# Second-layer output tiles in two tag groups, and one block of the second DFT in other PSUM banks

## The chip, the cores and the metric

The kernel runs on one core of a Trainium2 chip. The core has five engines that work through their own instruction streams in order: TensorE (PE, matrix products), VectorE (DVE), ScalarE (ACT), GpSimd (POOL) and SyncE (SP, which here only issues transfers). They wait for one another through semaphores. On-chip memory is SBUF, 128 partitions wide; matrix products go to PSUM, used here in units called banks (one bank holds 128 x 512 values of 4 bytes). The metric is the device time of one execution in microseconds (us); lower is better.

## What is computed

The reference is one transformer-like block with two branches, on a sequence of 4096 tokens with 640 channels:

```python
h = _layernorm(x) * (1 + ca) + sa
x = x + ga * _A_ref(h, A_w1, A_b1, A_w2, A_b2)     # spectral branch
h = _layernorm(x) * (1 + cb) + sb
x = x + gb * _B_ref(h, B_w_gate, B_w_up, B_w_down) # SwiGLU FFN
```

where `sa, ca, ga, sb, cb, gb` come from `silu(c) @ w_mod`, and the spectral branch is

```python
Xf = rfft2(x, axes=(1, 2))                  # H is 1: a 4096-point real DFT per channel
z  = Xf.reshape(B, H, Wf, NB, BS)           # 4 blocks of 160 channels
hr = zr @ w1[0] - zi @ w1[1] + b1[0]        # complex layer 1, per block; then ReLU
hi = zi @ w1[0] + zr @ w1[1] + b1[1]
or_ = hr @ w2[0] - hi @ w2[1] + b2[0]       # complex layer 2, per block
oi_ = hi @ w2[0] + hr @ w2[1] + b2[1]
...
mr = abs(or_) - lam                         # soft threshold, lam = 0.01
or_ = sign(or_) * mr * (mr > 0)
...
irfft2(or_ + 1j * oi_)
```

The change concerns the spectral branch alone.

## The kernel before

**Stages.** The 4096-point DFT is split as 128 x 32. In the first stage the x tiles (`xa0` to `xa7`, 128 partitions x 4 x 640 values, 10,240 bytes per partition each) are normalised and transformed over the 128 direction by TensorE; the results go back into the same x tiles and from there to memory (`write_s1`, lines 352 and 355; line 355 is used for tiles 6 and 7 only). Those writes are in three groups (f = 0, 1, 2), since different frequency chunks need different rows. The order in which they are issued on SP's queue is written out by hand: group 0 first, then group 1, then group 2, where tiles 6, 7 and 0 come last, in this order.

In the second stage the frequencies are done in 8 chunks of 256 (chunk 4 has 258), each with 4 blocks of 160 channels. A chunk's rows are loaded (`load_g`), and then, for each block t, come:

- `stage_b(ch, t)`: the second DFT, over the 32 direction, 32 small matmuls into PSUM. Channels 0 to 127 of each block are t = 0 to 3; the remaining 32 channels of all four blocks are t = 4, "the remainder".
- `evac_b(ch, t)`: ACT writes the scaled result as a rounded high part of z, DVE writes the low part (lines 679, 681). If the result lies in one bank-pair tile this is one operation on each engine, otherwise one for each of two banks.
- `evac_r(ch, b)`: in chunks 0 and 1, the remainder of one block is read out of (ch, 4) by two ACT operations (line 703) and two DVE operations (line 713).
- `stage_l1`, `tail_l1`: the first complex layer (line 774), ReLU by ACT (lines 791, 792), the low parts by DVE, and the remainder's own part (lines 805, 806, 815, 816).
- `stage_l2`: the second layer, 8 matmuls into one bank for each of two halves q of the frequencies (line 842), and then the addition of the bias by DVE into the output tile `tt` (line 844; 854 for the very first block). One output tile (2,560 bytes per partition) holds two blocks of one half, so a chunk needs four.
- `shrink_parts`, `shrink`: the soft threshold; ACT writes a scratch tile `cl` (line 862) and the tile itself (line 863), DVE subtracts (line 866).
- `stage_i(ch, hf)`: the inverse DFT over 32 (line 884), evacuated by ACT into the `co` tiles (line 887) and written to memory `s2`.

A last inverse DFT over 128 and the second layer norm form the start of the FFN part, which takes the rest of the time, from about 340 us on.

**Order.** All of this runs under a manual schedule: each engine does its instructions in the order of the program. `first_blocks` does the first chunk and the beginning of the second. Then comes a loop over steps p, with ch = p // 4 and b = p % 4; steps 0 to 3 only do small things (step 3 the first `shrink_parts`), and from p = 4 on each step does `shrink` of an earlier tile, `stage_l1` of block p, `stage_b` and `evac_b` of a later block, `tail_l1`, an inverse DFT, `stage_l2` of block p - 1 and `shrink_parts`. Step 4 thus holds the first layer of chunk 1's block 0, the second DFT of (1, 3), and the second layer of chunk 0's block 3.

**PSUM.** Tags `p1`, `p2` and `p3` have two banks each. A further pair, `bb`, is one tile in which t = 0 and t = 4 of a chunk share the space; t = 1, 2 and 3 otherwise take a whole `bb` tile each. Only four combinations of chunk and block, those named in `stage_b`, use `p2` or `p3`. `stage_l2` also writes to `p2`.

**SBUF.** The x tiles are in a pool on the right-hand side of SBUF, directly below the first layer's weights. When the x pool is closed, pool `p2` is opened at the same upper end, with tiles in this order of first use: `acc`, `cl` (2,560 bytes per partition each), `wx` (512), `bx` (1,024), the three weight tiles `w2a`, `w2b`, `w2c` (10,240 each), `tt` (6 buffers of 2,560), `wm` (2,560), `co` (4 of 2,560) and `xn` (2 of 2,560). A tile that lies on bytes of an earlier tile waits until the last use of those bytes is over, and only for the tiles that it overlaps. `acc` is the running sum of a modulation product, `bx` the matrix of the inverse DFT, `wm` a slice of `w_mod`. Their loads and the f = 2 writes stand in SP's one queue, first the writes, then `idn`, `tx`, `bx` (line 545) and `wm` (line 552). POOL makes the high parts of `w2a` and `w2b` (line 279).

When the FFN starts, its own pool takes over the same bytes; among its first tiles is `hx` (written by ACT at line 1930, and used by DVE at line 1933).

Of the kernel before, what the change touches and what calls it, by code (L numbers as in the profile page):

```python
# [6 lines left out]
F32 = mybir.dt.float32  # L7
# [6 lines left out]
P = 128  # L14
D = 640
# [153 lines left out]
def body(tc, x, w1, b1, w2, b2, wg, wu, wd, c, wm, k_fa, k_tb, k_tx, k_bx, k_ga, k_ge, k_id, out, dbg=None):  # L169
# [29 lines left out]
    with ExitStack() as top:  # L199
# [36 lines left out]
        with ExitStack() as af:  # L236
# [293 lines left out]
            p2 = af.enter_context(tc.tile_pool(name="p2", bufs=1, side="right", reuse_waits="tile"))  # L530
# [95 lines left out]
            tts = {}  # L626
# [24 lines left out]

            def stage_b(ch, t):
                g, tb = gs[ch], tbs[ch]
                tag = {(0, 1): "p2", (0, 2): "p3", (1, 1): "p3", (1, 2): "p2"}.get((ch, t))
                if tag:
                    banks = [ps.tile([P, 2, 128], F32, tag=tag, name=f"pb{ch}_{t}_{p}") for p in range(2)]
                else:
                    if t not in (0, 4) or (ch, 4 - t) not in bts:
                        bts[ch, t] = bp.tile([P, 2, 2, 2, 128], F32, tag="bb", name=f"pb{ch}_{t}")
                        k = 0  # L660
                    else:
                        k = 1
                    bt = bts[ch, 4 - t if k else t]
                    banks = [bt[:, p, k] for p in range(2)]
                    pairs[ch, t] = bt[:, :, k].rearrange("c p r k -> c p (r k)")
                pb = banks
                for j in range(4):
                    for d in range(2):
                        for p in range(2):
                            h, q = slice(64 * p, 64 * p + 64), slice(64 * d, 64 * d + 64)  # L670
                            mm(banks[p][q, :, 32 * j:32 * j + 32], g[h, j, 128 * t + 64 * d:128 * t + 64 * d + 64], tb[h, j, :],
                               start=True, stop=True)
                pbs[ch, t] = pb
# [15 lines left out]
            def evac_r(ch, b, part=None):  # L689
                if part != 1:  # L690
                    evac_rh(ch, b)
                if part != 0:
                    evac_rl(ch, b)
# [126 lines left out]
            def stage_l2(ch, b, then=()):  # L820
                h0, h1, r2, _ = hss[ch, b]
                late = []
                de = slice(160 * (b % 2), 160 * (b % 2) + 160)
                for q in range(3 if ch == CE else 2):
                    fs = slice(128 * q, 128 * q + 128) if q < 2 else slice(256, 258)
                    M = 128 if q < 2 else 2
                    W = 320 if q < 2 else 160
                    if b % 2 == 0 and q < 2:
                        tts[ch, q, b // 2] = p2.tile([P, 2, 320], F32, tag="tt", bufs=6, name=f"tt{ch}_{q}_{b // 2}")
                    pc = ps.tile([P, 512], F32, tag="p2" if q < 2 else "p1", name=f"pc{ch}_{b}_{q}")  # L830
                    seq = [(h0[:, 0, fs], w2a[:, b, 0:W]), (h0[:, 1, fs], w2a[:, b, 0:W]),
                           (h0[:, 0, fs], w2a[:, b, 320:320 + W]),
                           (h1[:, 0, fs], w2b[:, b, 0:W]), (h1[:, 1, fs], w2b[:, b, 0:W]),
                           (h1[:, 0, fs], w2b[:, b, 320:320 + W]),
                           (r2[:, fs], w2c[:, b, 0:W]), (r2[:, fs], w2c[:, b, 320:320 + W])]
                    if (ch, b) == (0, 0):
                        late.append((pc, [seq[k] for k in (2, 5, 7)]))
                        for i, k in enumerate((0, 1, 3, 4, 6)):
                            mm(pc[:M, :W], *seq[k], start=(i == 0), stop=False)
                        continue  # L840
                    for i, (l, m) in enumerate(seq):
                        mm(pc[:M, :W], l, m, start=(i == 0), stop=(i == len(seq) - 1))  # L842
                    if q < 2:
                        dve.tensor_tensor(tts[ch, q, b // 2][:, :, de], pc[:, :320].rearrange("p (r e) -> p r e", r=2),
                                          b2t[:, :, b, :], op=OP.add)
                        if then:
                            then[q]()
                    else:

                        dve.tensor_tensor(tts[ch, 0, b // 2][0:1, 1, de], pc[0:1, :160], b2t[0:1, 0, b, :], op=OP.add)  # L850
                for q, (pc, seq) in enumerate(late):
                    for i, (l, m) in enumerate(seq):
                        mm(pc[:, :320], l, m, start=False, stop=(i == 2))
                    dve.tensor_tensor(tts[ch, q, b // 2][:, :, de], pc[:, :320].rearrange("p (r e) -> p r e", r=2),
                                      b2t[:, :, b, :], op=OP.add)

            cos = {}
# [14 lines left out]
            def stage_i(ch, hf, tag=("p1", "p1", "p3", "p3")):  # L872
                e = slice(320 * hf, 320 * hf + 320)
                if hf == 0:
                    cos[ch] = [p2.tile([P, D], F32, tag="co", bufs=4, name=f"co{ch}_{j}") for j in range(4)]
                co = cos[ch]
                pi = [bank0(0, [P, 512], f"pi{ch}_{hf}_{j}") if tag[j] == "b0" else
                      ps.tile([P, 512], F32, tag=tag[j], name=f"pi{ch}_{hf}_{j}") for j in range(4)]
                for r in range(2):
                    for q in range(2):  # L880
                        for j in range(4):
                            k = slice(32 * j, 32 * j + 32)
                            kd = 0 if 4 * ORDER[ch] + j + q == 0 else 1
                            mm(pi[j][64 * q:64 * q + 64, :320], bx[k, kd, r, :], tts[ch, q, hf][k, r, :],
                               start=(r == 0), stop=(r == 1))
                for j in range(4):
                    act.activation(co[j][:, e], pi[j][:, :320], AF.Copy)  # L887
                    m = 4 * (4 * ORDER[ch] + j)
                    if ch == NCH - 1:
                        (pool if hf else nc.scalar).dma_start(s2[m:m + 4, :, e].rearrange("k n d -> (k n) d"), co[j][:, e])  # L890
                    elif hf:
                        pool.dma_start(s2[m:m + 4].rearrange("k n d -> (k n) d"), co[j])  # L892
# [77 lines left out]
            for p in range(LAST + 1):  # L970
                ch, b = p // 4, p % 4
                if p == 0:
                    first_blocks()
                if p < 4:
                    for f, *a in mods.get(p, ()):
                        f(*a)
                    on(shrink_parts, p - 3)
                    continue
                on(shrink, p - 4)
                on(stage_l1, p)  # L980
                if b == 0:
                    todo = [(ch, 3)]
                else:
                    todo = [(ch + 1, 4)] * (b == 1) + [(ch + 1, b - 1)]
                todo = [q for q in todo if q[0] < NCH]
                if p == 4:
                    evac_r(1, 2)
                    evac_r(1, 3)
                for q in todo:
                    stage_b(*q)  # L990
                    if q[1] < 4:
                        evac_b(*q)
                for f, *a in sums.get(p, ()):
                    f(*a)
                if b == 1 and ch + 1 < NCH:
                    rem_high(ch + 1)
                on(tail_l1, p)
                if b == 1 and ch + 1 < NCH:
                    rem_low(ch + 1)
                    rem_move(ch + 1)  # L1000
                if b == 2 and ch + 1 < NCH:
                    rem_read(ch + 1)
                inverse(p - 5)
                on(stage_l2, p - 1)
                on(shrink_parts, p - 3)
                if b == 3 and 2 < ch + 2 < NCH:
                    load_g(ch + 2)
                    load_tb(ch + 2)
                for f, *a in mods.get(p, ()):
                    f(*a)  # L1010
                if p == LAST - 4:
                    cf += [rp.tile([P, 2, D], F32, tag=tag, name=f"cf{tag}") for tag in ("rm", "rr")]
                    load_first_rows(rb + 16, rl, nc.sync)
                elif p == LAST - 1:
                    load_first_rows(0, rb - 16, nc.sync)
# [1548 lines left out]
```

## Time and profile before

| | us |
|---|---|
| median of 3 runs | 1472.26 |
| lowest and highest run | 1471.22, 1476.57 |
| the profiled execution | 1470.01 |
| its span, first to last instruction | 1468.2 |

The share of the span in which each engine is busy is 89% for the weight loads of TensorE, 74% for VectorE, 53% for ScalarE and 37% for GpSimd; TensorE's matmuls are in the rows below. The mean granted clock of TensorE is 0.987 of full speed.

Rows of the timeline begin with the time from the span's start and the duration, then the engine, the line of the kernel, the operation, output <- input by the program's names, and the count; in square brackets stands how long the engine had been idle and what ended that. Rows of the windows give a stretch and its length, then for each engine the busy time and the count, then the granted clock, the busy share of the DMA engines and the GB/s that they moved. In the chain of waits a row is a time, a duration and what took it, and in the queue view the last number is the median time in us from issue to landing. A matmul's duration in the timeline includes its way through the pipeline, so successive rows overlap; the distance between starts is what one costs.

### The profile page before, as it was taken

How to read it: one execution, taken by the hardware profiler on the slowest of the kernel's cores; microseconds unless marked ns; L12 is line 12 of the kernel's file. 1: busy time of each engine (PE TensorE's matmuls, PEld its weight loads, DVE VectorE, ACT ScalarE, POOL GpSimd, SP SyncE). 2: the span in 40 equal slices, each digit the busy share in tenths (PEclk: the TensorE clock that was granted, in tenths of full speed). 3: DMA queues.
4: the chain of work that ended last, by engine and by line, in shares of the span. 5: the costliest groups of instructions: out<-in, count | busy, mean ns of one | idle time of the engine just before them, and what ended most of it. 6: DMA issues, size and time to landing. Idle time of an engine off the chain costs nothing.

```text
span 1468.2 us, 26387 instructions
## 1 busy us (share of the span) xinstructions
PE 1404.3 (96%) x9788; PEld 1308.1 (89%) x9788; DVE 1085.3 (74%) x1961; ACT 772.9 (53%) x1552; POOL 538.8 (37%) x640
## 2 busy tenths in 40 slices
PE   7859999988999999999999999999999999999999
PEld 2548888966888888999999999999999999999998
DVE  8747687766887788758788868788737767667775
ACT  7737777735554465535565545555625434344432
POOL 5200022014344345413344424444314545145542
PEclk9989999998999999999999999999999999999999
DMA  9865587754766998899777897877896666967552
GB/s 373 291 188 143 166 229 230 233 179 155 254 229 223 333 318 258 288 381 308 255 255 267 307 390 247 298 247 269 281 363 222 221 210 219 374 211 246 203 171 99
DMA packets 182977, 371.95 MB, mean 253 GB/s; under 512 B 21536, under 2 KB 105056, under 8 KB 181056
## 3 DMA queue, kind: packets, MB, share of 16 engines
q1 hardware_dynamic: 174800, 354.14, 71.1%
q0 software_dynamic: 6464, 13.50, 2.8%
q10 hardware_dynamic: 1584, 2.62, 0.5%
q8 instruction: 77, 1.26, 0.3%
q14 instruction: 52, 0.43, 0.1%
HBM read 265.35 MB, written 104.86 MB: 252 GB/s over the span
## 4 chain that ended last, share of the span: by engine, by line
PE 80%; DVE 10%; DMA 4%; ACT 2%; issue 1%; POOL 1%; SPq 0%; ACTq 0%; DVEq 0%; POOLq 0%
PE pd L2434 15%; PE pw L2115 8%; PE pw L2117 8%; PE pw L2116 8%; PE pc L842 5%; PE pd_X L2296 5%; PE pl L774 4%; PE pg L1979 3%; PE pg L1980 3%; PE pg L1981 3%; PE pd_Y L2296 2%; PE pw L2126 2%; PE pw L2128 2%; PE pw L2127 2%; DVE st_a L190 2%; PE py L1701 2%
## 5 line engine op out<-in xcount | busy, mean ns | idle before, releaser
L2434 PE MATMUL pd<-wdh,a 128*128 128x320 f32 x1040 | 239.2, 310 | 1.1 <-DVE x L2406 1.1
L2434 PEld LDWEIGHTS pd<-wdh,a 128*128 128x128 f32 x1040 | 176.2, 188 | 1.8 <-DVE x L2406 1.4
L2434 PE MATMUL pd<-wdl,a 128*128 128x320 f32 x540 | 166.2, 309 | 0.0
L1456 DVE TENSOR_TENSOR wb<-r,wb 128x512 fp32r<-128x512 f32 (+3 forms) x154 | 152.8, 1003 | 14.9 <-ACT wb L1453 13.5
L2115 PE MATMUL pw<-h,wt 128*128 128x384 f32 x416 | 141.2, 339 | 2.2 <-ACT s_x L2134 2.2
L2117 PE MATMUL pw<-h,wt 128*128 128x384 f32 x416 | 140.2, 337 | 0.0
L2116 PE MATMUL pw<-h,wt 128*128 128x384 f32 x416 | 139.9, 336 | 0.0
L2406 DVE TENSOR_TENSOR x<-x,pd 128x320 f32<-128x320 f32 x240 | 109.7, 480 | 37.3 <-PE pd L2434 33.2
L1453 ACT ACTIVATE wb<-r 128x512 fp32r<-128x512 f32 (+3 forms) x170 | 117.4, 704 | 33.4 <-PE pw L2128 24.8
L2115 PE MATMUL pw<-h,wb 128*128 128x384 f32 x312 | 105.1, 337 | 0.9 <-DVE x L2406 0.9
L2116 PE MATMUL pw<-h,wb 128*128 128x384 f32 x312 | 104.7, 335 | 0.0
L2117 PE MATMUL pw<-h,wb 128*128 128x384 f32 x312 | 104.6, 335 | 0.0
L1979 PE MATMUL pg<-ht,wb 128*128 128x512 f32 x260 | 102.3, 393 | 0.0
L2434 PEld LDWEIGHTS pd<-wdl,a 128*128 128x128 f32 x540 | 101.4, 188 | 0.3
L1980 PE MATMUL pg<-ht,wb 128*128 128x512 f32 x260 | 101.4, 390 | 0.0
L1981 PE MATMUL pg<-ht,wb 128*128 128x512 f32 x260 | 101.4, 390 | 0.0
L2134 ACT ACTIVATE s_x<-pw 128x384 f32<-128x384 f32 x52 | 25.4, 488 | 119.9 <-PE pw L2117 118.8
L1684 POOL TENSOR_TENSOR cr<-cr,gab 128x640 f32<-128x640 f32 x28 | 48.2, 1724 | 95.4 <-DMA cr<-s 80.0
L2115 PEld LDWEIGHTS pw<-h,wt 128*128 128x128 f32 x416 | 78.1, 188 | 3.6 <-ACT s_x L2134 3.5
L2116 PEld LDWEIGHTS pw<-h,wt 128*128 128x128 f32 x416 | 78.2, 188 | 0.0
L2117 PEld LDWEIGHTS pw<-h,wt 128*128 128x128 f32 x416 | 78.1, 188 | 0.0
L892 POOL DMA_DIRECT2D s<-co x28 | 15.5, 555 | 169.5 <-ACT co L887 168.7
(348 smaller groups left out, 3966.3 us busy)
## 6 DMA issues: line engine op xcount, KB each, us to landing
wt<-td SPq DMA_DIRECT2D x104, 512.0 KB, 5.2
hs<-ho SPq DMA_DIRECT2D x52, 512.0 KB, 5.3
h<-hs SPq DMA_DIRECT2D x32, 768.0 KB, 8.7
r<-in_B_w_up_dram SPq DMA_DIRECT2D x36, 640.0 KB, 4.7
r<-in_B_w_gate_dram SPq DMA_DIRECT2D x36, 640.0 KB, 4.7
wdr<-wdd SPq DMA_DIRECT2D x25, 640.0 KB, 5.6
td<-wt SPq DMA_DIRECT2D x25, 512.0 KB, 5.8
g<-s SPq DMA_DIRECT2D x14, 640.0 KB, 8.5
```

The costliest lines, as they stand in the source:

```text
L842: mm(pc[:M, :W], l, m, start=(i == 0), stop=(i == len(seq) - 1))
L1453: act.activation(wbs[t, n][:, 0, ks, e], raw[t, n][:, ks, e], AF.Copy)
L1456: (pool if onp else dve).tensor_tensor(wbs[t, n][:, 1, ks, e], raw[t, n][:, ks, e], f32(wbs[t, n][:, 0, ks, e]), op=OP.subtract)
L1979: mm(b, wh, hh, start=(kk == 0), stop=False)
L1980: mm(b, wh, hl, start=False, stop=False)
L1981: mm(b, wl, hh, start=False, stop=(kk == 4))
L2115: mm(b, w(0, kp), a[:, kp, 0], start=start and kp == 0, stop=False, skip_group_check=not start)
L2116: mm(b, w(0, kp), a[:, kp, 1], start=False, stop=False, skip_group_check=not start)
L2117: mm(b, w(1, kp), a[:, kp, 0], start=False, stop=kp == 1, skip_group_check=not start)
L2296: mm(bk[b, i][:, :320], x, y, start=new and j == 0, stop=j == len(seq) - 1, skip_group_check=not new)
L2406: dve.tensor_tensor(x2[:, e], x2[:, e], x[0][:, :320], op=OP.add)
L2434: mm(pd[g, hf][0][:, :320], l, m, start=i == 0, stop=i == len(s) - 1 and not (last and len(gs) > 1))
```

## The change

There are four edits:

1. `stage_b`: (chunk 1, block 3) gets the tag `p2`, and so two single banks in place of the pair `bb`.
2. `stage_l2`: the output tiles have the tag `tt` in even chunks and `tu` in odd ones, each with 4 buffers, where one tag had 6.
3. `stage_i`: tag `co` has 5 buffers in place of 4.
4. In step 4 the remainder of chunk 1's blocks 2 and 3 is read out after the second DFT of (1, 3) and its evacuation, where it was read out before them.

```diff
@@ stage_b
-                tag = {(0, 1): "p2", (0, 2): "p3", (1, 1): "p3", (1, 2): "p2"}.get((ch, t))
+                tag = {(0, 1): "p2", (0, 2): "p3", (1, 1): "p3", (1, 2): "p2", (1, 3): "p2"}.get((ch, t))
@@ stage_l2
-                        tts[ch, q, b // 2] = p2.tile([P, 2, 320], F32, tag="tt", bufs=6, name=f"tt{ch}_{q}_{b // 2}")
+                        tts[ch, q, b // 2] = p2.tile([P, 2, 320], F32, tag=("tt", "tu")[ch % 2], bufs=4, name=f"tt{ch}_{q}_{b // 2}")
@@ stage_i
-                    cos[ch] = [p2.tile([P, D], F32, tag="co", bufs=4, name=f"co{ch}_{j}") for j in range(4)]
+                    cos[ch] = [p2.tile([P, D], F32, tag="co", bufs=5, name=f"co{ch}_{j}") for j in range(4)]
@@ the loop over steps
-                if p == 4:
-                    evac_r(1, 2)
-                    evac_r(1, 3)
                 for q in todo:
                     stage_b(*q)
                     if q[1] < 4:
                         evac_b(*q)
+                if p == 4:
+                    evac_r(1, 2)
+                    evac_r(1, 3)
```

The computation itself is unchanged: the same operations on the same values.

## The prediction

> **What bounds the kernel now.** I read the page first, then the windows, then the timeline around each hole. One row of the page, and the stages:
>
> ```profile
> PE 1404.3 (96%) x9788; PEld 1308.1 (89%) x9788; DVE 1085.3 (74%) x1961; ACT 772.9 (53%) x1552; POOL 538.8 (37%) x640
> ```
>
> ```profile
> 80.53:92.67 12.14, 0.00 (x0) 0.00 (x0) 0.54 (x2) 0.00 (x0) 0.00 (x0) 0.71 0.89 247
> 92.67:98.00 5.33, 5.33 (x33) 5.20 (x37) 2.98 (x7) 1.34 (x4) 0.00 (x0) 0.71 0.76 286
> 106.90:112.65 5.75, 0.06 (x2) 0.01 (x1) 3.86 (x8) 3.54 (x9) 0.00 (x0) 0.72 0.00 0
> 112.65:117.20 4.55, 4.55 (x48) 4.43 (x49) 1.66 (x3) 2.54 (x4) 0.00 (x0) 0.60 0.02 4
> 117.20:163.00 45.80, 45.80 (x661) 40.88 (x665) 34.30 (x67) 36.24 (x77) 2.41 (x4) 1.00 0.60 160
> 163.00:318.00 155.00, 148.38 (x1888) 131.11 (x1871) 111.26 (x207) 109.94 (x241) 28.94 (x49) 0.99 0.72 213
> 338.50:347.00 8.50, 3.66 (x9) 2.13 (x9) 4.61 (x3) 6.04 (x9) 5.94 (x8) 0.68 0.56 166
> 347.00:376.00 29.00, 29.00 (x127) 24.18 (x128) 23.81 (x33) 15.21 (x26) 8.63 (x7) 0.92 0.62 196
> ```
>
> TensorE is busy for 96% of the span, so time can only be won where it stands still. The windows (stretch, length, then busy time of PE, PEld, DVE, ACT, POOL, granted clock, DMA share) show three holes near the edit: 12.14 us without a matmul, 5.75 us with next to none, and 8.50 us at the start of the FFN with 3.66 busy. From 117.20 to 163 and from 347 to 376 TensorE is busy throughout: what is won before these stretches travels through them, and most of what follows is of the same kind. VectorE's timeline, TensorE's, and the chain of waits name what ends the first hole:
>
> ```profile
> 92.13 0.49 DVE L854 TENSOR_TENSOR tt<-pc,b2t 128x320 f32<-128x320 f32 x1 [13.09 <-DMA s<-xa]
> ```
>
> ```profile
> 92.67 1.17 PE L842 MATMUL pc<-w2a,h 128*128 128x320 f32 x3 [12.15 <-DVE tt L854]
> 93.64 1.00 PE L842 MATMUL pc<-w2b,h 128*128 128x320 f32 x3
> ```
>
> ```profile
> 83.27 8.77 DMA s<-xa
> ```
>
> **First hole.** The bias addition of the second output tile (L854) sat 13.09 us until a copy out of an x tile had landed; TensorE waited 12.15 us behind it for a PSUM bank. The chain shows the copy: issued at 83.27, 8.77 us long, so landed at 92.04.
>
> Which x tile follows from counting bytes per partition upwards from the bottom of the x pool, where x tile t covers 10,240t to 10,240(t+1). p2 ends at the same top, and its tags lie upwards in order of first use. It has 70,656 B, so it starts at 81,920 - 70,656 = 11,264: acc there, cl at 13,824, then wx, bx and the weights up to 48,640, six output tiles from 48,640 to 64,000 (x tiles 4 and 5 and the foot of 6), wm, the co tiles from 66,560 to 76,800, xn. One output slot of six lies on x tile 6, whose last copy is late; the second tile got it, as the 13.09 us show.
>
> **Second hole.** ScalarE's timeline, then the chain of waits:
>
> ```profile
> 105.03 0.83 ACT L862 ACTIVATE cl<-tt,nlam 128x640 f32<-128x640 f32 x1
> ...
> 108.21 0.38 ACT L805 ACTIVATE u<-pl 64x256 f32<-64x256 f32 x1
> 108.61 0.95 ACT L703 ACTIVATE rz<-pb,ca 32x256 fp32r<-32x256 f32 x2
> ```
>
> ```profile
> 112.10 0.50 DVE rz L713
> 112.60 0.04 issue
> 112.65 1.14 PE pb L671 x32
> 113.78 3.70 PE pc L842 x16
> 117.48 2.49 PE pl L774 x21
> ```
>
> Block (1,3) needs the one bank pair bb, which two remainder pieces of chunk 1 are still read out of: ACT's pair at 108.61, DVE's pair, ACT's again, DVE's again, until 112.60. Only then come its 32 matmuls and the second layer (3.70 us).
>
> **The change, part by part.** *Tags.* p2 gets two output tiles and one co tile more: 3 x 2,560 = 7,680 B, so it starts at 3,584. Upwards: acc, cl at 6,144 to 8,704, wx, bx at 9,216 to 10,240, then w2a, w2b, w2c exactly on x tiles 1, 2 and 3; tt at 40,960 to 51,200, exactly x tile 4; wm; co from 53,760 to 66,560; tu from 66,560 to 76,800, exactly where co was. (co is first used at step 5 before tu is.) SP's timeline and, for the last of the first row's four issues, the queue:
>
> ```profile
> 57.06 2.83 SPq L352 DMA_DIRECT2D s<-xa  x4
> ```
>
> ```profile
> s<-xa SPq DMA_DIRECT2D x1, 640.0 KB, 10.6
> ```
>
> The last copy out of x tile 4 was issued before 59.89 and took 10.6 us: landed by 70.5, before the first bias addition. The wait at L854 goes, and TensorE's 12.15 us with it. What is late next? The same two views for the last copy of all, out of x tile 0:
>
> ```profile
> 86.65 0.77 SPq L352 DMA_DIRECT2D s<-xa  x1
> ```
>
> ```profile
> s<-xa SPq DMA_DIRECT2D x1, 640.0 KB, 8.8
> ```
>
> It lands at 86.65 + 8.8 = 95.45, and on x tile 0 now lie acc, cl, wx and bx. cl is the scratch of the soft threshold, first written by L862, the 105.03 row. ACT works in order, so it now waits at L862 until 95.45; behind it stand L863, the first-layer evacuations of block (1,0), the z pieces of (1,3), and for these TensorE's second layer of block (0,3). Would L862 have been ready earlier? 12.15 us earlier it stands at 92.9. The clock after the hole was 0.71, so some 5.33 x 0.29 = 1.5 us more may go. And the weights move:
>
> ```profile
> 66.18 3.62 POOL L279 TENSOR_SCALAR w2a<-rm 128x640 fp32r<-128x640 f32 x2 [24.85 <-DMA s<-xa]
> ```
>
> ```profile
> 74.80 0.57 PE L839 MATMUL pc<-w2b,h 128*128 128x320 f32 x2 [2.91 <-POOL w2b L279]
> ```
>
> POOL's copies into w2a began when a copy out of an x tile had landed; w2a now lies on x tile 1 alone, long free, so up to the 2.91 us that TensorE waited for w2b goes. L862 is ready between 88.5 and 92.9: the new wait binds, and what is won ahead of it does not show. L862 at 95.5 instead of 105.03: **9.5 us**.
>
> bx's load waits in SP's queue for the same copy, and both wm loads stand behind it:
>
> ```profile
> bx<-in_k_bx_dram SPq DMA_DIRECT2D x1, 128.0 KB, 5.1
> ```
>
> bx lands at about 95.5 + 5.1 = 100.6, its user (the first inverse DFT) comes after 107; the wm loads are issued right behind it, and their first sum stands behind the second layer, past 104. Cost nothing under these covers; beyond them, the overrun.
>
> *Two other banks, remainder later.* Block (1,3) now writes two p2 banks, free once the z pieces of (1,2) are done, so its matmuls run while ACT waits. L862 to the second layer's start was 113.78 - 105.03 = 8.75 us. Now it is L862 to the end of L805, 108.59 - 105.03 = 3.56, and the first of two z pieces on ACT and DVE:
>
> ```profile
> 60.84 0.84 ACT L679 ACTIVATE z<-pb,ca 128x256 fp32r<-128x256 f32 x2
> ```
>
> ```profile
> 61.35 0.88 DVE L681 SCALAR_TENSOR_TENSOR z<-pb,ca,z 128x256 fp32r<-128x256 f32 x2
> ```
>
> DVE's first starts 0.51 after ACT's first and takes half of 0.88 with some overlap, so 1.0 in all: 4.55 instead of 8.75, **4.2 us**, and the second layer starts at 100.05. The remainder's four pairs, 0.95 each, follow on ACT and DVE to about 104; bb's next user, chunk 2's block 4, comes after the second layer and the next first layer (3.70 + 2.49), at 106. They also push back the tail of the first layer, two bias additions and the next threshold, but all that TensorE needs of these stands behind the same 6.2 us of matmuls. I count 0, bounds 0 and -1.0 (one pair showing).
>
> *Clock.* TensorE now stands once, from about 90 to 100, and starts slow there, as in the 0.60 stretch; but there the 1.14 us of block (1,3) took part of the slow time. All 16 matmuls at the pace of the first three after the first hole, (93.64 - 92.67)/3 = 0.32, would take 5.2 against 3.70: bounds 0 and -1.5; I take **-0.5**, a third, since the slow time ended within that stretch.
>
> *Fifth co tile.* Nothing. The closest meeting of two chunks' co tiles is here, and ACT waits for itself:
>
> ```profile
> 315.67 0.44 ACT L887 ACTIVATE co<-pi 128x320 f32<-128x320 f32 x1 [0.46 <-ACT we L1035]
> ```
>
> *Start of the FFN.* ACT, DVE and POOL:
>
> ```profile
> 337.66 0.78 ACT L1927 ACTIVATE ht<-pt,sb,cb 128x512 fp32r<-128x512 f32 x1 [1.28 <-PE pt L1925]
> 340.93 0.78 ACT L1930 ACTIVATE hx<-pt,sb,cb 128x512 f32<-128x512 f32 x1 [2.49 <-DMA s<-co]
> ```
>
> ```profile
> 341.74 0.69 DVE L1933 TENSOR_TENSOR ht<-hx,ht 128x512 fp32r<-128x512 f32 x1 [4.50 <-ACT hx L1930]
> 343.08 3.86 DVE L1933 TENSOR_TENSOR ht<-hx,ht 128x512 fp32r<-128x512 f32 x1 [0.65 <-ACT hx L1930]
> ```
>
> ```profile
> 338.98 0.74 POOL L1500 TENSOR_TENSOR ts<-r 128x256 f32<-128x256 f32 x1
> ...
> 344.85 1.53 POOL L1684 TENSOR_TENSOR cr<-cr,gab 128x640 f32<-128x640 f32 x1
> ```
>
> hx waited 2.49 us for the last copy out of a co tile. On those bytes lies tu now, read last by the inverse DFT, before 337; hx follows L1927 at once, TensorE's wait on DVE behind it shrinks: **2.5 us**. Bounds 0 (its users held elsewhere) and 2.49 + 3.17 = 5.7: the second difference took 3.86 where the first took 0.69, beside POOL's additions up to 346.4, and would now come before most of these. The Trainium skill, "SBUF — State Buffer", section "SBUF: two separate sides", says that a VectorE operation with two SBUF inputs and a GpSimd operation exclude one another for a whole instruction. By it the first difference, now due at 339.2, would wait for POOL's 338.98 row to end at 339.72 and give 2.0 instead of 2.5 there, and 3.17 more at the second. The 3.86 row agrees with it.
>
> **Sum.** 9.5 + 4.2 - 0.5 + 2.5 = 15.7 us. The profiled execution took 1470.01 (span 1468.2), so 1454.3. The median of the runs shown is 1472.26, 2.25 above it: **1456.6**.
>
> **Rivals.** *The scratch wait does not bind.* For: the copy is only 2.5 to 7 us behind ACT. Against: its place in SP's order is unchanged. The gain is then 15.7 + 2.5 to 7, about 20: 1452. *Part is given back.* From 163 to 318 there are 155.00 - 148.38 = 6.6 us of holes which need not shift with the rest, and the FFN term can be 0. With 2.5 and another 2.5 lost the gain is 10.7: 1461.5. *The change does not do what it says:* tags lie otherwise and the second output tile stays on a late x tile; then at most 4.2 + 2.5 remain, 1466. Against: the count for before puts the waiting tile right. *Slower:* the copy out of x tile 0 lands far later than 95.45, and each us costs one at L862. From 95.45 + 15.7 = 111 on the kernel is slower, with a landing at 120 by 9 us: 1481. Against: 8.8 us now, 10.6 in the fullest stretch.
>
> **How the numbers follow.** Forecast 0.58, wait not binding 0.12, given back 0.20, not as said 0.06, slower 0.04. 0.5% is 7.4 us, about what a measurement of this kernel can tell. The first three are faster, less 0.02 for a larger giving back: 0.88; same 0.08; slower 0.04. The range: the forecast's terms at their bad bounds give 15.7 - 1.0 - 1.0 - 2.5 = 11.2, at the good ones 15.7 + 0.5 + 3.2 = 19.4; widened towards the rivals beside it, 10.3 to 23.3: 1449 to 1462.
>
> **What would show it.** No wait before L854; L862 waiting for a copy out of x until about 95.5; block (1,3) done before that; the second layer of (0,3) some 4.5 us after L862; no DMA wait at hx. Wrong would be L862 without that wait, a wait at bx, or a hole after 104 ended by a remainder piece.

## The result

| | us |
|---|---|
| before, median of 4 runs beside it | 1473.78 |
| after, median of 4 runs | 1455.62 |
| lowest and highest run after | 1452.59, 1457.40 |
| ratio after / before, 95% interval | 0.9874 [0.9848, 0.9901] |
| profiled execution after, and its span | 1452.59, 1450.8 |

The change is 1.3% faster; predicted were 1456.6 us. The page after, to set beside the row of before:

```profile
PE 1400.4 (97%) x9788; PEld 1306.8 (90%) x9788; DVE 1083.5 (75%) x1962; ACT 773.3 (53%) x1553; POOL 534.5 (37%) x640
```

TensorE was busy 1404.3 us before and 1400.4 after, so of the 17.4 us by which the span fell (1468.2 to 1450.8) 13.5 were idle time of TensorE, and 3.9 a quicker pace of its work. First the timelines of VectorE, ScalarE and SyncE after, then the chain of waits:

```profile
76.78 0.94 DVE L854 TENSOR_TENSOR tt<-pc,b2t 128x320 f32<-128x320 f32 x2 [0.57 <-PE pc L853]
```

```profile
88.74 0.84 ACT L679 ACTIVATE z<-pb,ca 128x256 fp32r<-128x256 f32 x2 [0.20 <-PE pb L671]
96.18 0.83 ACT L862 ACTIVATE cl<-tt,nlam 128x640 f32<-128x640 f32 x1 [6.60 <-DMA s<-xa]
```

```profile
96.17 0.33 SPq L545 DMA_DIRECT2D bx<-in_k_bx_dram  x1
96.55 0.91 SPq L552 DMA_DIRECT2D wm<-in_w_mod_dram  x2
```

```profile
87.04 9.12 DMA s<-xa
```

The two first bias additions (L854) now follow one another without a wait for a transfer. In its place ScalarE stands 6.60 us at L862, until the copy that was issued at 87.04 has landed 9.12 us later, at 96.16. In SyncE's queue the load of `bx`, whose bytes lie under the same x tile, goes out at 96.17, within 0.01 us of L862: both wait for the same transfer. The hole in TensorE's work behind that wait (timeline, then windows):

```profile
91.31 0.69 PE L671 MATMUL pb<-tb,g 64*64 64x64 f32 x32
100.80 1.17 PE L842 MATMUL pc<-w2a,h 128*128 128x320 f32 x3 [8.79 <-DVE z L681]
...
104.54 0.52 PE L774 MATMUL pl<-z,w1a 128*128 128x256 f32 x3
...
108.22 1.55 PE L884 MATMUL pi<-tt,bx 32*64 32x320 f32 x32
```

```profile
91.95:100.80 8.85, 0.06 (x4) 0.00 (x1) 2.58 (x6) 4.51 (x10) 0.00 (x0) 0.78 0.63 219
```

Block (1,3), the row at 91.31, is done before the wait ends; then the two holes of before (12.14 and 5.75 us) have become one of 8.85. The start of the FFN after, from ScalarE's, VectorE's and GpSimd's timelines:

```profile
325.28 0.78 ACT L1927 ACTIVATE ht<-pt,sb,cb 128x512 fp32r<-128x512 f32 x1 [1.28 <-PE pt L1925]
325.96 0.77 ACT L1930 ACTIVATE hx<-pt,sb,cb 128x512 f32<-128x512 f32 x1
```

```profile
326.76 1.13 DVE L1933 TENSOR_TENSOR ht<-hx,ht 128x512 fp32r<-128x512 f32 x1 [1.90 <-ACT hx L1930]
328.10 0.94 DVE L1933 TENSOR_TENSOR ht<-hx,ht 128x512 fp32r<-128x512 f32 x1 [0.20 <-ACT hx L1930]
329.44 1.57 DVE L1933 TENSOR_TENSOR ht<-hx,ht 128x512 fp32r<-128x512 f32 x1 [0.40 <-ACT hx L1930]
```

```profile
326.60 0.74 POOL L1500 TENSOR_TENSOR ts<-r 128x256 f32<-128x256 f32 x1
327.42 1.07 POOL L1500 TENSOR_TENSOR ts<-r,ts 128x256 f32<-128x256 f32 x1
```

`hx` no longer waits, and the second difference takes 0.94 us where it took 3.86. The longest of the five is now the third, with 1.57 us. One more row is needed, of TensorE before, the start of the second layer of block (0,3):

```profile
113.71 1.17 PE L842 MATMUL pc<-w2a,h 128*128 128x320 f32 x3
```

The whole gain, measured between the starts of the same instructions in the two profiled executions:

| from | before | after | gained |
|---|---|---|---|
| span's start to L862 | 105.03 | 96.18 | 8.85 |
| L862 to the second layer of block (0,3) | 8.68 | 4.62 | 4.06 |
| from there to the first inverse DFT (L884) | 7.28 | 7.42 | -0.14 |
| from there to L1927 | 216.67 | 217.06 | -0.39 |
| L1927 to the first matmul of L1979 | 16.73 | 10.84 | 5.89 |
| from there to the end of the span | 1113.81 | 1114.68 | -0.87 |
| sum | | | 17.40 |

L1979 is the group of matmuls behind the first 30 of the FFN (L1939 to L1941). Between the edits and the FFN, and after it, 0.39 and 0.87 us were given back.

### The profile page after: what moved, and what is told of

Its sections match the earlier page's. It is cut to its first block, busy times and chain, and to the rows that moved or that the text cites. A ratio compares the mean times of both kernels' runs of the same rounds, so it can differ in the third digit from the quotient of the medians.

```text
span 1450.8 us, 26385 instructions
## 1 busy us (share of the span) xinstructions
PE 1400.4 (97%) x9788; PEld 1306.8 (90%) x9788; DVE 1083.5 (75%) x1962; ACT 773.3 (53%) x1553; POOL 534.5 (37%) x640
## 3 DMA queue, kind: packets, MB, share of 16 engines
q8 instruction: 77, 1.26, 0.3%
## 4 chain that ended last, share of the span: by engine, by line
PE 77%; DVE 10%; DMA 6%; ACT 3%; issue 2%; POOL 1%; SPq 1%; DVEq 0%; ACTq 0%; POOLq 0%
PE pd L2434 14%; PE pw L2115 8%; PE pw L2117 8%; PE pw L2116 8%; PE pd_X L2296 5%; PE pc L842 5%; PE pl L774 4%; PE pd_Y L2296 2%; PE pg L1980 2%; PE pg L1981 2%; PE pg L1979 2%; PE pw L2126 2%; PE pw L2128 2%; PE pw L2127 2%; PE pi L884 1%
## 5 line engine op out<-in xcount | busy, mean ns | idle before, releaser
L1456 DVE TENSOR_TENSOR wb<-r,wb 128x512 fp32r<-128x512 f32 (+3 forms) x154 | 156.3, 1026 | 12.7 <-ACT wb L1453 11.2
L1979 PE MATMUL pg<-ht,wb 128*128 128x512 f32 x260 | 102.3, 394 | 0.0
L2270 DVE TENSOR_TENSOR x<-x,pd_X 128x320 f32<-128x320 f32 x144 | 64.4, 483 | 14.3 <-PE pd_X L2296 14.3
```

The lines of the kernel that those rows point to most:

```text
L1456: (pool if onp else dve).tensor_tensor(wbs[t, n][:, 1, ks, e], raw[t, n][:, ks, e], f32(wbs[t, n][:, 0, ks, e]), op=OP.subtract)
L1979: mm(b, wh, hh, start=(kk == 0), stop=False)
```

## The experiments

My theory: three things were won, each in its own place. The output tiles moved off a late x tile, and the wait that replaces the old one is that of the scratch tile `cl` on x tile 0; block (1,3) no longer waits for the remainder; and the FFN's start is freed of a copy out of `co` and falls otherwise against GpSimd's work. Rivals: another wait (of `bx`, of the weights, of the output tiles) sets L862; what is won there is given back later; the slow difference at the FFN's start has another cause than GpSimd. All times are medians, all ratios are to the runs of the kernel before on the same chip (medians 1473.13 to 1473.78). The last three columns, and the spans, are of each kernel's one profiled execution.

| | us | ratio, 95% interval | L862 | inverse DFT | L1927 to L1979 |
|---|---|---|---|---|---|
| before | 1473.78 | | 105.03 | 120.99 | 16.73 |
| after | 1455.62 | 0.9874 [0.9848, 0.9901] | 96.18 | 108.22 | 10.84 |
| e1 tags only | 1458.23 | 0.9899 [0.9883, 0.9914] | 97.36 | 113.38 | 10.85 |
| e2 banks and order only | 1466.65 | 0.9952 [0.9938, 0.9967] | 105.17 | 117.45 | 16.58 |
| e3 scratch elsewhere | 1447.14 | 0.9824 [0.9807, 0.9841] | 88.34 | 99.10 | 11.12 |
| e4 x tile 0 written first | 1452.77 | 0.9850 [0.9827, 0.9874] | 94.11 | 107.05 | 10.85 |
| e5 names by half | 1456.63 | 0.9884 [0.9857, 0.9912] | 97.83 | 110.77 | 11.63 |
| e6 four `co` tiles | 1456.69 | 0.9891 [0.9868, 0.9915] | 96.19 | 108.50 | 11.65 |
| e7 = e3 and e4 | 1447.86 | 0.9823 [0.9799, 0.9848] | 88.49 | 99.26 | 10.28 |
| e8 = e5, GpSimd cleared | 1453.51 | 0.9867 [0.9845, 0.9889] | 97.78 | 110.10 | 11.12 |
| e9 = before, GpSimd cleared | 1470.23 | 0.9986 [0.9966, 1.0006] | 108.38 | 124.84 | 14.09 |
| e10 = e7, GpSimd cleared | 1444.65 | 0.9819 [0.9789, 0.9849] | 90.11 | 100.89 | 8.90 |

**e1: the tags and the fifth `co` tile alone.** Edits 1 and 4 of the change are undone:

```diff
-                tag = {(0, 1): "p2", (0, 2): "p3", (1, 1): "p3", (1, 2): "p2", (1, 3): "p2"}.get((ch, t))
+                tag = {(0, 1): "p2", (0, 2): "p3", (1, 1): "p3", (1, 2): "p2"}.get((ch, t))
...
+                if p == 4:
+                    evac_r(1, 2)
+                    evac_r(1, 3)
                 for q in todo:
```

> Only the new tags and buffer counts; block (1,3) in bb and the remainder ahead of it, as before. Theory (the tags give the first gain up to the copy out of x tile 0, and the FFN's; banks and order give 4 us of their own): L862 waits for that copy until about 96.2 as in the changed kernel, the second layer of block (0,3) starts 8.7 us after L862 instead of 4.6, so 4.1 us slower than the changed kernel, about 1459.7. Rival (banks and order are hidden behind the scratch's wait): 1455.6, as the changed kernel.

Its timeline of TensorE:

```profile
104.96 1.13 PE L671 MATMUL pb<-tb,g 64*64 64x64 f32 x32 [13.95 <-DVE rz L713]
106.03 1.17 PE L842 MATMUL pc<-w2a,h 128*128 128x320 f32 x3
```

1458.23 us. Block (1,3) waits for the remainder's pieces again, and the second layer follows L862 by 106.03 - 97.36 = 8.67 us instead of 4.62. Its span is 5.1 us longer than that of after; 4.05 of it is this distance and 1.18 L862, since the copy of this run landed later. The medians differ by 2.6 us where 4.1 were expected, and the intervals of the two overlap, so it is the rows that show this part, not the times.

**e2: the banks and the order alone.** Edits 2 and 3 are undone:

```diff
-tag=("tt", "tu")[ch % 2], bufs=4
+tag="tt", bufs=6
...
-tag="co", bufs=5
+tag="co", bufs=4
```

> Only block (1,3) in p2 and the remainder after it; tags and buffer counts as before. Theory: L854 waits 13 us as before, L862 comes at 105, the second layer of (0,3) 4.6 us later instead of 8.7, hx waits 2.5 us for a co copy as before: 4.1 us faster than the kernel before, about 1469.7. Rival (the second layer must now wait for the z pieces in its own banks, and what stands behind the remainder is late): no gain, 1473.8.

Its VectorE and TensorE:

```profile
91.96 0.49 DVE L854 TENSOR_TENSOR tt<-pc,b2t 128x320 f32<-128x320 f32 x1 [12.48 <-DMA s<-xa]
```

```profile
109.79 1.04 PE L842 MATMUL pc<-w2a,h 128*128 128x320 f32 x3 [2.09 <-DVE z L681]
```

1466.65 us. The old wait is back, L862 starts at 105.17, and the second layer follows 4.62 us later: the bank term by itself is 8.68 - 4.62 = 4.06 us. At the inverse DFT 3.54 are left, and at the FFN `hx` waits 2.48 us as before. The spans of e1 and e2 fell by 12.3 and 3.4, together 15.7, where the whole change took 17.4, 1.2 of the rest being e1's later copy: in the spans the parts add up. The medians say so less sharply: e2 is 7.05 us faster than before there, more than the 4.1 expected, and e1 and e2 together 22.5 against 18.2 for the whole change, which the intervals still allow. Where e2's other 3 us come from is open; the profiled execution of before is itself 3.7 us below the median that e2 is held against.

**e3: the scratch tile elsewhere.** `cl` is put on bytes that no x tile ever had:

```diff
-            cl = p2.tile([P, D], F32, name="cl")
+            cl = None
...
+                nonlocal cl
+                if cl is None:
+                    cl = hp.tile([P, D], F32, name="cl")
```

> The changed kernel with the scratch cl in bytes that no x tile had; acc, wx and bx stay on x tile 0. Theory (only L862's wait for the last copy binds): L862 at about 89.6 without a wait, the second layer of (0,3) at about 94.2, less slow clock since TensorE stands only 2 us; 6 to 7 us faster than the changed kernel, about 1449. Rival (the next thing on x tile 0, bx or the sum in acc, takes the wait's place): the first inverse DFT waits for bx until about 98.5 to 101, gain 0 to 3, 1453 to 1455.6.

Three lines are added, so L862 is L865 here and L884 is L887. ScalarE, then TensorE:

```profile
88.34 0.83 ACT L865 ACTIVATE cl<-tt,nlam 128x640 f32<-128x640 f32 x1
```

```profile
92.96 0.71 PE L842 MATMUL pc<-w2a,h 128*128 128x320 f32 x3 [2.10 <-DVE z L681]
...
95.43 0.52 PE L774 MATMUL pl<-z,w1a 128*128 128x256 f32 x3
...
99.10 1.06 PE L887 MATMUL pi<-tt,bx 32*64 32x320 f32 x6
101.10 1.32 PE L887 MATMUL pi<-tt,bx 32*64 32x320 f32 x26 [0.94 <-DVE u L806]
```

1447.14 us, faster than both kernels by times whose intervals do not meet. L862 does not wait; it was ready at 88.34, while `bx` and `wm` were still loaded as late as in after (SyncE issued `bx` at 95.21 here). So `cl` was the tile that held the kernel, and `bx`, `wm` and the weights were not. The second layer is 7.84 us earlier than in after and takes 95.43 - 92.96 = 2.47 us instead of 104.54 - 100.80 = 3.74: behind a hole of 2.10 us TensorE is at full pace at once here (granted clock 1.00 in these matmuls), behind the 8.79 of after it is not (0.62). The length of the hole alone does not decide this: in e6 (and likewise in e2) the same matmuls took 3.99 us at a clock of 0.57 behind a hole just as short:

```profile
100.82 1.10 PE L842 MATMUL pc<-w2a,h 128*128 128x320 f32 x3 [2.09 <-DVE z L681]
...
104.81 0.52 PE L774 MATMUL pl<-z,w1a 128*128 128x256 f32 x3
```

TensorE had stood for the second output tile earlier on in e6 (4.41 us) and in e2 (10.48), and not in e3; whether that is the reason is not shown. In e3 what is late next shows too: 0.94 us in the inverse DFT, behind the remainder's pieces that were pushed back.

**e4: x tile 0 written out ahead of tiles 6 and 7.**

```diff
-            for t in (6, 7, 0):
+            for t in (0, 6, 7):
```

> The changed kernel with the last group of copies in the order x tile 0, 6, 7 instead of 6, 7, 0. Theory (L862 is released by this one copy): its issue moves from 87.0 to 83.6, so L862 starts near 92.7 instead of 96.2, 3.5 us faster, about 1452. Rival (the copies share the queue and all land together at its end): L862 stays near 96, 1455.6.

```profile
94.11 0.83 ACT L862 ACTIVATE cl<-tt,nlam 128x640 f32<-128x640 f32 x1 [4.46 <-DMA s<-xa]
```

```profile
98.74 1.17 PE L842 MATMUL pc<-w2a,h 128*128 128x320 f32 x3 [6.66 <-DVE z L681]
...
103.17 0.71 PE L774 MATMUL pl<-z,w1a 128*128 128x256 f32 x3
```

1452.77 us; the intervals of e4 and after overlap, so the times cannot tell the two apart. L862 (ScalarE's row above; TensorE's follow it) comes 2.07 us earlier: the copy was issued at 84.77 instead of 87.04, and L862 follows its landing as the theory says, but this is 2.07 us where the theory had 3.5. Half of it was gone at the inverse DFT (1.17 left): the second layer took 103.17 - 98.74 = 4.43 us at a lower clock (0.50 against 0.62 in after). At L1927 nothing was left.

**e5: names by half instead of by chunk.** All output tiles stay on x tiles 4 and 5, but the `co` tiles lie under `hx` again:

```diff
-tag=("tt", "tu")[ch % 2]
+tag=("tt", "tu")[b // 2]
```

> The changed kernel with one difference: the two names of the output tiles go by the half of the four blocks (first pair of blocks, second pair) instead of by the chunk. Then all output tiles still lie on x tiles 4 and 5, cl on x tile 0, but the combine's output tiles co lie again where hx starts. Theory (the FFN start is won by hx no longer waiting for a copy out of co, and with it by VectorE's differences falling otherwise against GpSimd's): the same as the changed kernel up to L1927 (325.3 us, L862 about 96), then hx waits about 2.5 us for a copy out of co, a VectorE difference lasts about 4 us again, and L1979 starts some 5 us later than the changed kernel's 336.1: about 1460.6 us. Rival (the FFN start gained for another reason, such as the clock or the earlier start of the stage): no such wait matters, 1455.6 us.

ScalarE and VectorE:

```profile
330.47 0.78 ACT L1930 ACTIVATE hx<-pt,sb,cb 128x512 f32<-128x512 f32 x1 [0.63 <-DMA s<-co]
```

```profile
331.28 3.75 DVE L1933 TENSOR_TENSOR ht<-hx,ht 128x512 fp32r<-128x512 f32 x3 [2.64 <-ACT hx L1930]
```

1456.63 us. A miss: the wait for a copy out of `co` came back, but with 0.63 us instead of 2.5, and the differences were held, but the longest took 1.82 us, where in before one took 3.86. The three of this row span 3.75 us, against 3.37 for three that nothing holds (e8, 329.63 to 333.00). L1927 to L1979 is 0.79 us longer than in after, not 5. The time lies nearer to the rival's; with five `co` tiles the last copy probably lies elsewhere, which I only argue. Since no difference of 4 us came about, the FFN's gain had to be tested where there is one, in the kernel before (e9).

**e6: four `co` tiles.**

```diff
-tag="co", bufs=5
+tag="co", bufs=4
```

> The changed kernel with four co tiles as before instead of five. The pool then starts 2,560 bytes higher and every tile of it shifts, cl still partly on x tile 0. Theory (the fifth tile only sets places; what is won or lost ahead of L862's wait does not show): L862 still waits for the copy out of x tile 0 until about 96, the end within 1.5 us of the changed kernel: 1455.6 us. Rival (the fifth tile is needed, by its place or by a later wait in the combine): slower by 3 us or more, 1459 or above.

Its VectorE and ScalarE:

```profile
83.17 0.49 DVE L854 TENSOR_TENSOR tt<-pc,b2t 128x320 f32<-128x320 f32 x1 [5.36 <-DMA s<-xa]
```

```profile
96.19 0.83 ACT L862 ACTIVATE cl<-tt,nlam 128x640 f32<-128x640 f32 x1
```

1456.69 us, the same as after. The places shifted. By the count one of the four places of `tt` (51,200 to 53,760) now lies on x tile 5, and 5.36 us of the old wait at L854 came back; yet L862 starts at 96.19 against 96.18. It waits for nothing there, since the work ahead of it ends just then, 0.3 us behind the copy (issued at 86.29, 9.6 us long, so landed at 95.9), which I had not foreseen: I expected it to wait still. This is the plainest row for the step that what is won or lost ahead of the scratch's wait does not show. In the times the fifth tile by itself brings nothing. At the FFN's start `hx` does not wait without it either; but there the fourth difference took 3.45 us beside three GpSimd operations without a gap, and L1927 to L1979 is 0.81 us longer than in after. Whether that comes from the missing tile or from how the operations happened to fall is not shown.

**e7: e3 and e4 together.**

> cl outside the bytes of the x tiles (as in e3) and x tile 0 written out ahead of 6 and 7 (as in e4). Theory (with cl elsewhere nothing that decides waits for x tile 0 any more, so the order of the copies only moves bx and wm forward): the same as e3, 1446 to 1447 us. Rival (the order still matters, through bx or through the load of the weights): better than e3 by over 2 us, 1445 or below.

1447.86 us, as e3: with `cl` elsewhere the order of the copies no longer matters. L862 starts at 88.49 and 88.34.

**e8: e5 with GpSimd cleared.** Five of GpSimd's operations beside the FFN's first differences go to VectorE, behind the differences:

```diff
-                        pool.tensor_tensor(s[:, o], a, b, op=OP.subtract)
+                        moved.append(o)
+                        (dve if len(moved) < 5 else pool).tensor_tensor(s[:, o], a, b, op=OP.subtract)
...
-                    pool.tensor_tensor(crs[r], crs[r], gab, op=OP.mult)
+                    gone.append(r)
+                    (dve if len(gone) < 2 else pool).tensor_tensor(crs[r], crs[r], gab, op=OP.mult)
```

> e5 with GpSimd's work beside the FFN's first differences taken away: the first four subtractions of L1500 and the first multiplication of L1684 are done by VectorE. Theory (the difference that lasts about 4 us is held back by GpSimd's operations beside it): hx still waits about 2.5 us, but the long difference of L1933 falls from about 4 to about 0.7 us, and L1979 starts about 3 us earlier than in e5, less what VectorE's five added operations take (0.7 us each) where they stand ahead of it. Rival (its length has another cause, such as the late hx itself): still about 4 us beside an idle GpSimd, L1979 not earlier than in e5.

Every difference takes 0.69 us now (lines shifted by four, L1933 is L1937); VectorE:

```profile
329.63 0.69 DVE L1937 TENSOR_TENSOR ht<-hx,ht 128x512 fp32r<-128x512 f32 x1 [2.62 <-ACT hx L1934]
330.97 0.69 DVE L1937 TENSOR_TENSOR ht<-hx,ht 128x512 fp32r<-128x512 f32 x1 [0.64 <-ACT hx L1934]
332.31 0.69 DVE L1937 TENSOR_TENSOR ht<-hx,ht 128x512 fp32r<-128x512 f32 x1 [0.65 <-ACT hx L1934]
```

The mechanism is as the theory has it; the size is not: from L1927 to L1979 only 0.51 us are won over e5, since e5 had no difference of 4 us to lose. The median, 1453.51 us, is 3.1 below e5's with intervals that overlap; in the profiles 1.6 of it is there already at the FFN's first row (327.43 against 329.06), ahead of the edit.

**e9: the kernel before, with GpSimd cleared.** The same five operations, moved in the kernel before.

> The kernel before the change, with one difference: GpSimd's first four subtractions of L1500 and its first multiplication of L1684 are done by VectorE, behind its differences. Theory (the 3.86 us of the second difference were GpSimd's operations beside it): hx still waits about 2.5 us for a copy out of co, the second difference takes 0.69 us instead of 3.86, and from L1941 to L1979 it is 8.2 us instead of 11.9, as in the changed kernel: 3.7 us less, 1470 us, up to 3 less than that if what e8 won over e5 later, between 484 and 623 us, comes too. Rival (the difference is late for another reason, such as the late hx): it still takes about 4 us, 1473.7 us.

ScalarE and VectorE:

```profile
345.48 0.78 ACT L1934 ACTIVATE hx<-pt,sb,cb 128x512 f32<-128x512 f32 x1 [2.51 <-DMA s<-co]
```

```profile
346.29 0.69 DVE L1937 TENSOR_TENSOR ht<-hx,ht 128x512 fp32r<-128x512 f32 x1 [4.52 <-ACT hx L1934]
347.63 0.69 DVE L1937 TENSOR_TENSOR ht<-hx,ht 128x512 fp32r<-128x512 f32 x1 [0.65 <-ACT hx L1934]
```

`hx` is as late as before, 2.51 us, and the second difference takes 0.69 us instead of 3.86: its length was GpSimd's operations beside it, not the late `hx`. L1927 to L1979 falls from 16.73 to 14.09, 2.64 of the 3.7 expected. (All of this execution runs some 4 us late from L862 on, ahead of the edit, so only distances are compared.) The times agree (2.9 us lower) but do not show it by themselves: the interval reaches 1.0006.

**e10: e7 with GpSimd cleared.**

> e7 (cl elsewhere, x tile 0 written out first) with the same five operations of GpSimd put on VectorE. Theory (at the FFN start e7's differences already cost TensorE little: L1927 to L1979 took 10.3 us there and takes 10.5 with the wait for hx of e8 left out): nothing at the start, and only if the 2.8 us that e8 won over e5 between 484 and 623 us belong to the moved operations and not to chance, 1445 us; else 1447.9. Rival (VectorE now becomes late for its weights behind the five added operations): slower than e7 by 1 us or more, 1449.

1444.65 us, the lowest median, but its interval overlaps those of e3 and e7, and its profiled span is 1445.5 against 1442.1 of e7. From L1927 to L1979 it is 8.90 us against 10.28; right behind, TensorE waits 1.14 us for a weight of VectorE's, so part of the rival came true as well. Whether the moved operations pay there stays open; that `cl` elsewhere pays (e3) does not.

## Why the prediction was right

- **First hole.** Right in its mechanism: no transfer is waited for at L854, L862 waits for the copy out of x tile 0 instead, and e3 shows that it is `cl` alone that waits with effect. Predicted 9.5 us, measured 8.85: the copy was issued at 87.04 instead of 86.65 and took 9.12 instead of 8.8 us. That this moved by less than 1 us is partly luck: with the same code ahead of it, the copy landed anywhere from 95.2 to 97.8 us in the profiled executions. What is won ahead does not show: L862 was ready at 96.18 - 6.60 = 89.6, within the 88.5 to 92.9 given; e6 lost that slack again and ended the same.
- **`bx` and `wm` behind the same copy.** Cost nothing, as said: e3 issues them as late and is 8.5 us faster than after, and e7 issues them earlier and is as fast as e3.
- **Two other banks, remainder later.** 4.2 predicted, 4.06 measured, and 4.06 and 4.05 by e2 and e1 alone. (The 8.75 of the prediction took 113.78 from the chain of waits, whose steps are laid end to end; in TensorE's timeline the second layer starts at 113.71, so 8.68.) The remainder cost nothing in after; the bound of 1.0 (a pair that shows) is what e3 shows, 0.94, once the wait is gone.
- **Clock.** -0.5 predicted; between the second layer and the inverse DFT -0.14 was measured, and -0.38 in e2 (7.66 us against 7.28). The size was a guess within its bounds, and it varies: the 16 matmuls took 3.60 us before, 3.74 in after, and 4.43 in e4 and e5. Nor can time be won only where TensorE stands still, as the prediction opens: 3.9 of the 17.4 us came from a quicker pace, 2.15 of them from L1941 to L1979, where its busy time fell from 10.32 to 8.17 us.
- **Fifth `co` tile.** Nothing in the times, as said (e6).
- **Start of the FFN.** This term was mis-sized: 2.5 us predicted, 5.89 measured, 0.2 above its upper bound of 5.7. I gave only the wait of `hx`. It fell by 2.59 (L1927 to L1930, 3.27 to 0.68), 0.43 was lost at the first difference, which took 1.13 us instead of 0.69 beside GpSimd, and 3.73 were won from L1941 to L1979 (11.90 to 8.17), where the second difference is no longer held. e9, with `hx` as late as before and GpSimd cleared, takes 9.24 there and so shows 2.66 of it. The other 1.07 went with a granted clock of 0.79 in after against 0.69 in e9; e8, where TensorE had stood for 1.38 us just before and not for 3.29 as in e9, has 8.17 and 0.79 too. The Trainium skill, "SBUF — State Buffer", section "SBUF: two separate sides", says that a VectorE operation with two SBUF inputs and a GpSimd operation that reads SBUF exclude one another, and that the one that starts first keeps the other out. The prediction's estimate by it was 2.0 + 3.17 = 5.2. The trace agrees that they exclude one another: beside an idle GpSimd every difference takes 0.69 us (e8, e9). Which of the two goes first it does not bear out everywhere: the 3.86 row of before starts at 343.08, ahead of GpSimd's 343.46, and was held all the same. (What the prediction calls GpSimd's additions are two subtractions and a multiplication.)
- **The rest.** Nothing was predicted for it; 0.39 and 0.87 us were given back, less than the 2.5 of the rival.

The sum, 15.7, was 1.7 below the span's 17.4: FFN +3.4, first hole -0.65, clock +0.4, banks -0.1, given back -1.26. That the time came within 1 us (1455.6 against 1456.6) is partly luck: by the medians the gain is 18.2 us, 2.5 more than the sum, and the runs of before beside it were 1.5 us slower than those that the forecast started from (1473.78 against 1472.26). Of the rivals, that of the wait that does not bind is what e3 builds on purpose: 1447.1, below the 1452 that I gave it: L862 gained 105.03 - 88.34 = 16.7 us there, just above the 9.5 + 7 allowed, 1.14 us came on top from the clock (second layer to inverse DFT, 6.14 us against 7.28), and the FFN's start gained 5.61 there too, not 2.5.

## What to carry to other kernels

When tiles are moved off late bytes, ask at once which tile now lies on the latest ones, and whether its first user needs it early: here a scratch tile of 2,560 bytes took over the wait, and 8 us more lay in putting it on bytes that no x tile had. A hole of TensorE can cost more than its length, since the matmuls behind it can start slow (2.47 us for 16 of them in e3, 3.74 to 4.43 behind the holes of after, e4 and e5); closing it can win both, but a short hole is no guarantee (e6). When an operation lasts several times its usual length, look at the engine beside it before you call it work.

## What was unexpected

- The same 128x512 subtraction of VectorE took 0.69 us beside an idle GpSimd (e8, e9), 0.69 to 1.57 in after, and 3.86 where three of GpSimd's followed one another without a gap (before; GpSimd's timeline):

```profile
342.88 0.57 POOL L1676 DMA_DIRECT2D gt<-in_k_ga_dram  x1 [2.36 <-issue]
343.46 0.74 POOL L1500 TENSOR_TENSOR ts<-r 128x256 f32<-128x256 f32 x1
344.15 0.73 POOL L1500 TENSOR_TENSOR ts<-r,ts 128x256 f32<-128x256 f32 x1
344.85 1.53 POOL L1684 TENSOR_TENSOR cr<-cr,gab 128x640 f32<-128x640 f32 x1
```

  It had started at 343.08, ahead of the first of the three at 343.46, while GpSimd issued a transfer, and ended 0.56 us after the last (344.85 + 1.53 = 346.38, against 346.94). The transfer alone does not hold it: in e8 the first difference, at 329.63, took 0.69 us while GpSimd issued transfers from 328.85 to 329.94. Why VectorE did not get in ahead of the first of the three stays open. In after GpSimd left 0.08 us between two operations (326.60 + 0.74 = 327.34, the next at 327.42), and VectorE got in between: there GpSimd's second operation took 1.07 us instead of 0.73. The lengthened second, third and fifth differences of after, and the 3.45 us one of e6, likewise end 0.54 to 0.56 us after the end of a GpSimd operation; that distance is the sign to look for.
- The last copy out of the x tiles, of 640 KB, landed between 95.2 us (e3) and 97.8 (e5) with the same code ahead of it, and L862 moved with it where it waits for it. In e4's order it landed at 94.0 (84.77 + 9.26). In e9's profiled execution L862 started 3.35 us later than in that of before, ahead of any edit. So a microsecond or two between two profiled executions tells nothing here; only distances within one stage do.
